# A fused Mamba-2 scan and low-rank mixer on one core: sums moved from GpSimd to VectorE, one tile's Strassen product made plain, dummy products merged, and weight loads held back

## The chip, the cores and the metric

The kernel runs on one NeuronCore of a Trainium2 chip. The metric is device time in microseconds (us) of one execution, as the median of several. Beside it stands the profile of one execution on the same kind of core, with the start and duration of every instruction on every engine: TensorE (PE, with its weight loads shown apart as PEld), VectorE (DVE), ScalarE (ACT), GpSimd (POOL), and the DMA issues of SyncE (SP). "Span" is the time from the first to the last instruction in that profile.

## What is computed

Two stages follow each other, in fp32. First a chunked state-space scan over 4 batches, 8 heads, 768 positions, head size 32 and state size 16:

```python
L = np.exp(cum[..., :, None] - cum[..., None, :]) * causal
y_intra = einsum('bhij,bhjd->bhid', (Cc @ Bc.T) * L, xc)
y_inter = einsum('bhin,bhnd->bhid', Cc, state) * exp(cum)[..., None]
state = exp(sum(la)) * state + sum_j(Bc_j xc_j * exp(cum[-1] - cum_j))
```

Then the heads are laid side by side, which gives x of 4 x 768 x 256, and a mixer with a residual follows:

```python
u = x + ((x.T @ U @ V).T)                 # mixing over the 768 positions, rank 32
out = u + np.maximum(u @ w_ch1, 0) @ w_ch2   # 256 -> 1024 -> 256
```

U, V and the two weight matrices arrive as 64-bit floats.

## The kernel before

**Staging.** The 768 positions of a batch are cut into 6 blocks of 128, taken as 3 pairs, so there are 12 pairs in all, numbered k = 0 to 11. For one pair the steps are `prep` (B and C times their decays, on DVE), `decayed` (POOL), `turn` (transposes to channel-major, copied out by ACT), `gram` (the C·B products, into four PSUM banks), `mask` (DVE, four pieces), `state` and `update` (the carried state; DVE, then POOL for the copy `Sm`), `inter` and `intra` (the two parts of y), `yout` (ACT), and `ytokens` (transposes back to position-major, copied out to `ytok`). After the three pairs of a batch the mixer of that batch runs: `project` (U), `mixed` (V, adds into u), then the product with w_ch1 and relu into `gT`, then the product with w_ch2 into `o` and the store, in three row tiles j = 0, 1, 2. The scan of batch b+1 runs between the pieces of batch b's mixer.

**Order.** The kernel opens a manual schedule: each engine runs its instructions in the order in which they are written. `plan`, `ups` and `downs` are lists of closures, and the main loop over k = 3 to 12 runs a list (`pieces`) between the steps of the scan.

**The two ways of multiplying.** For batch 0 the first product is plain: `up(k, m)`, two 128x384 products each, 16 of them. For batches 1 to 3 it is a seven-product Strassen scheme, `quad`, with pieces p1 to p7. It needs combined weights `ws`. The second product, `down(j)`, is Strassen for every batch: seven products of four 128x128 steps, with combined weights `w2s` and four DVE/POOL combinations S of the activations, made by `sums` (line 671). `operands` (line 922) makes `w2s` and `ws`, eight tensor ops of 128x512, on POOL, after the pairs k = 3, 4 and 5.

**Weights.** They are loaded as 64-bit words and turned into fp32 by `to_fp32`, in two halves of DVE and ACT instructions. `convert_ahead` runs the second half of one weight tile and the first half of the next; ten calls are spread by hand over the first part of the program. Tiles are U, V, four quarters of w1 (512 KB each) and four quarters of w2. All loads are issued by SP in one order: three pairs of B, C and x; U; V; w1's quarters; pair 3; w2's quarters; pairs 4 to 11. Six `words` buffers are shared, so that w2's loads wait for conversions.

**Dummy products.** `warm` and `fill` put products of the identity with itself, 128x128 each, in front of chosen steps, so that TensorE stays active during the first pairs, where it has little to do.

**Extra edges.** `behind` remembers an ACT or DVE instruction, and `inter(k, 1)` is made to wait for it.

## Time and profile before

| what | value |
|---|---|
| time, median of 3 | 256.12 us (255.63 to 256.95) |
| span of the profiled execution | 253.7 us |
| mean TensorE clock granted | 0.992 |
| PE busy | 234.6 us |
| DVE busy | 151.9 us |
| ACT busy | 96.1 us |
| POOL busy | 50.3 us |

The shares are averages over quite different stretches. In the first 25 us three pairs of batch 0 are scanned while data and weights arrive. From 35 to 70 us the weights are converted while batch 0's first product and batch 1's scan run. After 100 us batches 1 to 3 run the same pattern.

### The profile page before, as it was taken

What the parts mean: (1) busy time and instruction counts of PE and PEld (TensorE: products, weight loads), DVE (VectorE), ACT (ScalarE), POOL (GpSimd) and SP (SyncE); (2) the same over time, 40 slices, a digit from 0 to 9 for tenths busy, and PEclk for the clock granted to TensorE, in tenths of its full rate; (3) what the DMA queues carried; (4) which work ended last, traced back from release to release, by engine and by line L of the source; (5) the groups of instructions that cost most, each with busy time, mean ns of one, the idle gap of its engine ahead of it and who ended that gap; (6) DMA issues with size and microseconds to landing.
All of it is one profiled execution on the core that took longest, in us unless ns stands there. A gap on an engine that the chain in (4) does not pass through costs nothing.

```text
span 253.7 us, 7506 instructions
## 1 busy us (share of the span) xinstructions
PE 234.6 (92%) x3222; PEld 180.9 (71%) x3222; DVE 151.9 (60%) x337; ACT 96.1 (38%) x248; POOL 50.3 (20%) x74
## 2 busy tenths in 40 slices
PE   7988689797978979999989999999999999999995
PEld 7866556454768868656579979565599986558995
DVE  3366579969697986257584935265582462447521
ACT  5345457557521301347532301536522113563110
POOL 4031000103471480004270200005320000051000
PEclk9999799999999999999999999999999999999999
DMA  6989796999875401100000110100001011000111
GB/s 79 113 120 285 126 276 118 128 111 102 99 97 64 88 1 44 41 0 4 0 5 0 48 40 4 41 3 1 3 3 44 3 41 41 3 0 0 41 45 41
DMA packets 81637, 14.60 MB, mean 58 GB/s; under 512 B 76036, under 2 KB 79556, under 8 KB 81604
## 3 DMA queue, kind: packets, MB, share of 16 engines
q1 hardware_dynamic: 81604, 14.13, 30.9%
q8 instruction: 25, 0.41, 0.7%
q14 instruction: 8, 0.07, 0.1%
HBM read 10.98 MB, written 3.15 MB: 56 GB/s over the span
## 4 chain that ended last, share of the span: by engine, by line
PE 77%; DVE 13%; ACT 4%; issue 3%; DMA 1%; POOL 0%; DVEq 0%; SPq 0%; POOLq 0%; ACTq 0%
PE x L682 16%; PE x L579 12%; PE z L682 11%; PE z L579 8%; PE y L498 4%; DVE words L671 3%; PE y L478 3%; PE x L216 2%; PE w L359 2%; PE w L537 2%; PE w L519 2%; PE x L377 2%; DVE yT L552 1%; PE x L548 1%; PE w L409 1%
## 5 line engine op out<-in xcount | busy, mean ns | idle before, releaser
L579 PE MATMUL x<-t,ws 128*128 128x384 f32 x72 | 29.2, 503 | 0.5 <-ACT top L584 0.5
L436 POOL TENSOR_TENSOR Sm<-S,slot 128x256 f32<-128x256 f32 (+1 forms) x12 | 9.8, 813 | 99.2 <-DVE S L429 83.3
L682 PE MATMUL x<-w2s,words 128*128 128x128 f32 x192 | 25.5, 275 | 0.0
L682 PEld LDWEIGHTS x<-w2s,words 128*128 128x128 f32 x192 | 23.6, 193 | 0.1
L579 PEld LDWEIGHTS x<-t,ws 128*128 128x128 f32 x72 | 12.4, 189 | 13.5 <-ACT top L584 4.9
L740 ACT COPY o<-x 128x128 f32<-128x128 f32 x12 | 3.2, 266 | 45.9 <-PE x L682 45.9
L567 ACT ACTIVATE gT<-gT 128x384 f32<-128x384 f32 x36 | 17.6, 523 | 5.9 <-DVE gT L588 5.3
L671 POOL TENSOR_TENSOR words<-gT 128x256 f32<-128x256 f32 (+1 forms) x12 | 8.2, 682 | 48.4 <-PE x L579 36.3
L671 DVE TENSOR_TENSOR words<-gT 128x512 f32<-128x512 f32 (+1 forms) x20 | 16.8, 839 | 0.6 <-ACT gT L567 0.6
L389 DVE TENSOR_TENSOR M<-x,causal 128x256 int32<-128x256 int32 x24 | 10.1, 420 | 11.5 <-PE z L377 11.4
L343 POOL TENSOR_TENSOR bd<-bc,FD 128x256 f32<-128x256 f32 (+1 forms) x13 | 9.9, 772 | 29.9 <-ACT FD L264 29.9
L682 PE MATMUL x<-w,gT 128*128 128x128 f32 x96 | 14.0, 287 | 1.8 <-issue 1.1
L682 PEld LDWEIGHTS x<-w,gT 128*128 128x128 f32 x96 | 11.9, 191 | 4.6 <-DVE yT L552 2.5
L682 PE MATMUL z<-w,words 128*128 128x128 f32 x96 | 12.8, 276 | 1.9 <-DVE words L671 1.9
L588 DVE TENSOR_TENSOR gT<-z,top 128x384 f32<-128x384 f32 x12 | 6.7, 558 | 11.2 <-PE z L579 9.3
L622 DVE TENSOR_SCALAR gT<-x 128x384 f32<-128x384 f32 x12 | 6.7, 558 | 11.1 <-PE x L579 11.1
L510 ACT COPY yT<-y 128x256 f32<-128x256 f32 x24 | 7.8, 377 | 14.3 <-PE y L478 14.3
L682 PE MATMUL z<-w2s,words 128*128 128x128 f32 x96 | 12.7, 276 | 0.5 <-DVE words L671 0.5
L682 PEld LDWEIGHTS z<-w,words 128*128 128x128 f32 x96 | 11.7, 192 | 2.1 <-DVE words L671 2.1
L682 PE MATMUL z<-w,gT 128*128 128x128 f32 x96 | 12.7, 275 | 0.0
L682 PE MATMUL x<-w2s,gT 128*128 128x128 f32 x96 | 12.7, 275 | 0.0
L642 PE MATMUL x<-yT,w 128*128 128x384 f32 x32 | 12.0, 496 | 0.7 <-DVE yT L552 0.6
(159 smaller groups left out, 527.2 us busy)
## 6 DMA issues: line engine op xcount, KB each, us to landing
words<-in_moe_w_ch_dram SPq DMA_DIRECT2D x8, 512.0 KB, 6.3
x<-in_x_dram SPq DMA_DIRECT2D x24, 128.0 KB, 3.3
out_dram<-o SPq DMA_DIRECT2D x11, 256.0 KB, 2.1
bc<-in_B_dram SPq DMA_DIRECT2D x24, 64.0 KB, 3.8
bc<-in_C_dram SPq DMA_DIRECT2D x24, 64.0 KB, 3.3
words<-in_moe_U_dram SPq DMA_DIRECT2D x1, 192.0 KB, 4.9
words<-in_moe_V_dram SPq DMA_DIRECT2D x1, 192.0 KB
out_dram<-o SPq DMA_DIRECT2D x1, 128.0 KB, 1.7
```

The lines of the kernel that those rows point to most:

```text
L343: nc.gpsimd.tensor_tensor(out=st[k]["bd"][:, c:c + n].rearrange("p c h n -> p (c h) n"), in0=bc_sb[k][:, 0, c:c + n].rearrange("p c h n -> ...
L389: done = nc.vector.tensor_tensor(out=M[:, r].bitcast(INT32).rearrange("p c s i -> p (c s) i"), in0=g[r].bitcast(INT32).rearrange("p c s i ...
L436: nc.gpsimd.tensor_tensor(out=s["Sm"][:, sl], in0=s["S"][:, sl].rearrange("p i (s d) -> p i s d", s=2), in1=slot[:, None, :, None].to_broa ...
L478: product = nc.tensor.matmul(out=y[p][ts(r % 2, H), r // 2, c], lhsT=own[ts(r, Q)], rhs=s["T"][ts(r, Q), 1, c, ts(p, H)], start=fresh(k, p ...
L498: nc.tensor.matmul(out=y[p][ts(i, Q), n, c], lhsT=x_sb[k][half, c, h], rhs=s["M"][half, h // 2, c, h % 2], start=fresh(k, p, [i]), stop=Tr ...
L510: nc.scalar.copy(out=yp[:, :, :, p], in_=st[k]["y"][p])
L567: nc.scalar.activation(g, g, AF.Relu)
L579: nc.tensor.matmul(out=X[name], lhsT=lhsT[:, ts(i, P)], rhs=rhs, start=start, stop=True, skip_group_check=True)
L588: nc.vector.tensor_tensor(out=g, in0=X[of], in1=X[other], op=ALU.add)
L642: nc.tensor.matmul(out=g, lhsT=w1[:, n, ts(m, P)], rhs=uT[:, n, ts(k, HS)], start=(n == 0), stop=(n == NCB - 1))
L671: engine.tensor_tensor(out=S[v][:, lo:hi], in0=l[:, lo:hi], in1=r[:, lo:hi], op=op)
L682: nc.tensor.matmul(out=X[name], lhsT=lhsT[:, i], rhs=rhs[:, i], start=start and u is None and i == 0, stop=True, skip_group_check=True)
```

## The change

It does six things. Dummy products of one call become one wide product. The loads from w1's third quarter on, and thus everything queued behind them on SP, wait for the last mask piece of pair 2. The j = 0 tile of batch 0's second product is made plain (`whole`: for each half, two transposes and eight 128x256 products, then one ACT copy), so it needs neither `w2s` nor S; `ahead` goes with it. `sums` and `operands` are all on DVE. The copy to `ytok` for batch 1 moves from DVE to ACT. And the hand-written order of batch 0 changes: conversions and `keep` move, all ten conversions end ahead of the main loop, and one set of two `up` products moves from the loop to before it. The purpose is that TensorE waits less for its operands, for GpSimd, and for loads.

```diff
+    def idle(t, n):
+        while n > 0:
+            m = min(n, max(t.shape[1] // P, 1), 4)
+            w = min(P, t.shape[1])
+            nc.tensor.matmul(out=t[:, :m * w].rearrange("p (m i) -> p m i", i=w), lhsT=ident,
+                             rhs=ident[:, None, :w].to_broadcast([P, m, w]), start=True, stop=True)
+            n -= m
...
-        for _ in range(fills[0]):
...
-            nc.tensor.matmul(out=flat[:, :n], lhsT=ident, rhs=ident[:, :n], start=True, stop=True)
+        if fills[0]:
+            idle(t if len(dims) == 1 else t.rearrange(
...
-    for k in range(DF // quarter):
-        load_words(w1[:, :, ts(k, quarter)],
+    held = [load_words(w1[:, :, ts(k, quarter)],
...
-        copy = nc.scalar.copy if b == 0 else nc.vector.tensor_copy
+        copy = nc.scalar.copy if b < 2 else nc.vector.tensor_copy
...
-                        engine = nc.gpsimd if b and j == 0 and lo < 3 else nc.vector
-                        engine.tensor_tensor(out=S[v][:, lo:hi], in0=l[:, lo:hi],
+                        nc.vector.tensor_tensor(out=S[v][:, lo:hi], in0=l[:, lo:hi],
...
+            def whole(k):
+                g = bank("x", DM)
+                for n in range(NCB):
+                    nc.tensor.matmul(
+                        out=g[:, ts(n, P)], lhsT=uT[:, n, ts(HT * k + j, P)], rhs=ident,
+                        is_transpose=True, start=(n == 0), stop=False, skip_group_check=True)
+                for half in range(2):
+                    for i in range(NM // 2):
+                        m = half * NM // 2 + i
+                        nc.tensor.matmul(out=g, lhsT=blocks()[k][half][:, i], rhs=w2[:, m],
+                                         start=False, stop=(m == NM - 1), skip_group_check=True)
...
+            if b == 0 and j == 0:
+                return sums, [lambda: whole(0), lambda: whole(1)]
...
-            plan = [[ups.pop(-2), ups.pop()], [ups.pop(-2), ups.pop()], downs.pop(0)]
+            plan = [[ups.pop(-2), ups.pop()]] + [[piece] for piece in downs.pop(0)]
...
-                plan[1].insert(2 * v, step(0, v, 0, 2))
-                plan[1].append(step(0, v, 2, 4))
+                plan[1].insert(6 + 2 * v, step(0, v, 0, 2))
+            plan[1] += [step(0, v, 2, 4) for v in range(4)]
...
-    mask(2, (1, 3))
+    tc.add_manual_dep(held[2].ins, mask(2, (1, 3)).ins.name, mybir.DependencyInfo(
+        mybir.DependencyClass.Sync, mybir.DependencyReason.DATA))
...
-    for _ in range(3):
+    for _ in range(2):
         some(2)
         convert_ahead()
     decays(others, "y")
     keep(others)
     prep(3)
     decayed(3)
+    some(2)
+    convert_ahead()
+    some(2)
+    convert_ahead()
+    prep(4)
+    decayed(4)
     some(2)
     turn(3)
     convert_ahead()
...
     update(3)
-    prep(4)
-    decayed(4)
+    convert_ahead()
     some(2)
     turn(4)
-    convert_ahead()
-    plan[0].append(convert_ahead)
...
-                pieces = pieces[:4] + tokens + pieces[4:]
+                pieces = pieces[:3] + tokens + pieces[3:]
...
-                          + late[11:] + (plan[0] if k < last else []))
+                          + late[11:] + [lambda: operands(4, nc.vector)] + (plan[0] if k < last else []))
...
-        if k == NPR + 1:
-            run(ahead)
-        if k < 2 * NPR:
-            operands((2, 2, 4)[k - NPR], nc.gpsimd)
+        if k < NPR + 2:
+            operands(2, nc.vector)
```

More of the change, by code (lines that the diff above doesn't have):

```diff
@@ L75 @@
     fills = [0]
+    def idle(t, n):
[5 more added lines that the diff above has]
+            n -= m
     def bank(tag, *dims):
         t = psum.tile([P, *dims], FP32, tag=tag, name=tag, bufs=BANKS[tag])
-        for _ in range(fills[0]):
-            flat = t if len(dims) == 1 else t.rearrange(
-                {2: "p a b -> p (a b)", 3: "p a b c -> p (a b c)"}[len(dims)])
-            n = min(P, flat.shape[1])
-            nc.tensor.matmul(out=flat[:, :n], lhsT=ident, rhs=ident[:, :n], start=True, stop=True)
+        if fills[0]:
+            idle(t if len(dims) == 1 else t.rearrange(
+                {2: "p a b -> p (a b)", 3: "p a b c -> p (a b c)"}[len(dims)]), fills[0])
         fills[0] = 0
@@ L144, in load_words @@
         t = words_of(dst)
-        nc.sync.dma_start(out=t.rearrange("p (i j) -> p i j", i=i), in_=src)
+        return nc.sync.dma_start(out=t.rearrange("p (i j) -> p i j", i=i), in_=src)
     U2, V2, w12, w22 = (w.bitcast(INT32) for w in (moe_U, moe_V, moe_w_ch1, moe_w_ch2))
@@ L155 @@
     quarter = WCOLS // NCB
-    for k in range(DF // quarter):
-        load_words(w1[:, :, ts(k, quarter)],
-                   w12[:, ts(k, 2 * quarter)].rearrange("(c p) m -> p c m", p=P))
+    held = [load_words(w1[:, :, ts(k, quarter)],
+                       w12[:, ts(k, 2 * quarter)].rearrange("(c p) m -> p c m", p=P))
+            for k in range(DF // quarter)]
     load_bc(3)
@@ L212, in warm @@
     def warm(n, tag="w"):
-        t = bank(tag, P)
-        for _ in range(n):
-            nc.tensor.matmul(out=t, lhsT=ident, rhs=ident, start=True, stop=True)
+        idle(bank(tag, 4 * P), n)
     warm(3, "x")
@@ L393, in mask @@
             behind.setdefault("part", done)
+        return done
     def chunks(k, c, n):
@@ L669, in sums @@
                     if v in which:
-                        engine = nc.gpsimd if b and j == 0 and lo < 3 else nc.vector
-                        engine.tensor_tensor(out=S[v][:, lo:hi], in0=l[:, lo:hi],
-                                             in1=r[:, lo:hi], op=op)
+                        nc.vector.tensor_tensor(out=S[v][:, lo:hi], in0=l[:, lo:hi],
+                                                in1=r[:, lo:hi], op=op)
             def times(name, tag, lhsT, rhs, start=True, u=None):
@@ L745, in p4 @@
                 del hold["o"]
+            def whole(k):
[9 more added lines that the diff above has]
+                                         start=False, stop=(m == NM - 1), skip_group_check=True)
+                to(k, 0)
+                behind.setdefault("part", nc.scalar.copy(out=hold["o"][:, k], in_=g))
+                if k:
+                    store(None, None)
+                    del hold["o"]
+            if b == 0 and j == 0:
+                return sums, [lambda: whole(0), lambda: whole(1)]
             return sums, [p1, p5, p6, p3, p7, p2, p4]
@@ L780, in mixer @@
         downs = [piece for pieces in downs for piece in pieces]
-        return project, mixed, ups, plan, downs, [step(0, v) for v in range(4)]
+        return project, mixed, ups, plan, downs
     halves = [half for w in weights for half in (to_fp32(*w),) * 2]
@@ L813 @@
     ytok[0] = mix.tile([P, NC, DM], FP32, tag="ytok", name="ytok")
-    project, mixed, ups, plan, downs, ahead = mixer(0)
+    project, mixed, ups, plan, downs = mixer(0)
     decays(one)
@@ L900 @@
     update(3)
-    prep(4)
-    decayed(4)
+    convert_ahead()
     some(2)
     turn(4)
-    convert_ahead()
-    plan[0].append(convert_ahead)
+    assert not halves
     ws = const.tile([P, 5, DF // 2], FP32)
@@ L933 @@
             if q:
-                pieces = pieces[:4] + tokens + pieces[4:]
+                pieces = pieces[:3] + tokens + pieces[3:]
             else:
                 late = downs
-                project, mixed, ups, plan, downs, _ = mixer(b - 1)
+                project, mixed, ups, plan, downs = mixer(b - 1)
                 pieces = (late[:1] + tokens + late[1:7] + [project] + late[7:11] + [mixed]
-                          + late[11:] + (plan[0] if k < last else []))
+                          + late[11:] + [lambda: operands(4, nc.vector)] + (plan[0] if k < last else []))
         if k == last:
```

## The prediction

> **What bounds the kernel now.** I read the page's busy times first, then who waits for whom on TensorE, then the idle stretches by window, then the timeline around each.

> ```profile
> PE 234.6 (92%) x3222; PEld 180.9 (71%) x3222; DVE 151.9 (60%) x337; ACT 96.1 (38%) x248; POOL 50.3 (20%) x74
> q8 instruction: 25, 0.41, 0.7%
> ```

> TensorE sets the end, so a saving is either PE work or PE idle time. The idle is 19.1 us of 253.7 in all. PE's own waits, longest first:

> ```profile
> PE x L443 <- issue: 2.4, 1, 2.4
> PE z L682 <- DVE words L671: 2.3, 2, 1.9
> PE w L359 <- ACT gT L647: 1.9, 1, 1.9
> PE x L216 <- POOL ident masks.py:199: 1.4, 1, 1.4
> PE x L678 <- DVE o L696: 1.3, 1, 1.3
> PE w L359 <- DVE BC L331: 1.3, 1, 1.3
> PE x L682 <- issue: 1.1, 1, 1.1
> ```

> All but the fourth lie where the change works. The two "issue" waits have no semaphore behind them. The 25 packets of queue 8 are 16 KB each; their start times in the trace give the cause. By count of PE records (6498), PE stood idle after its 962nd (25.18 us) and after its 3778th (130.01 us), exactly 11 x 256 apart: these are ends of blocks of 256 instructions. [...] PE can go on some 1.35 us after it ends. At 130 us: block entered 127.62, packet 128.58 to 129.81, PE on at 131.16. At 25 us: block entered 20.33, but the packet started only at 25.22, with all four quarters of w1 already in the DMA rings. The windows show what follows (columns: PE, PEld, DVE, ACT, POOL busy, clock, DMA share):

> ```profile
> 25.20:27.60 2.40, 0.00 (x0) 0.00 (x0) 2.33 (x8) 1.04 (x3) 0.00 (x0) 1.00 1.03 252
> 27.60:31.20 3.60, 3.58 (x109) 2.97 (x113) 0.83 (x3) 1.32 (x5) 0.00 (x0) 0.54 0.52 55
> 47.60:49.60 2.00, 0.10 (x2) 0.08 (x2) 1.97 (x5) 0.76 (x3) 0.88 (x1) 1.00 0.97 96
> 60.80:62.20 1.40, 0.13 (x2) 0.10 (x2) 1.40 (x3) 1.34 (x4) 0.00 (x0) 1.00 1.05 99
> 92.60:94.00 1.40, 0.10 (x2) 0.09 (x2) 1.40 (x3) 0.00 (x0) 1.40 (x2) 1.00 0.00 0
> ```

> The stall costs twice: 2.45 us of nothing, then 3.4 us at half the clock. In the next two gaps DVE is full. In the last one, and at 75 us, DVE is full because POOL slows it:

> ```profile
> 72.85 1.71 POOL L922 TENSOR_TENSOR w2s<-w 128x512 f32<-128x512 f32 x1
> 73.36 1.75 DVE L671 TENSOR_TENSOR words<-gT 128x512 f32<-128x512 f32 x1
> 74.53 1.70 POOL L922 TENSOR_TENSOR w2s<-w,w2s 128x512 f32<-128x512 f32 x1
> 75.03 1.74 DVE L671 TENSOR_TENSOR words<-gT,words 128x512 f32<-128x512 f32 x1
> ```

> The same DVE instruction alone takes 0.69 us.

> [...] the clock record here has half clock from 27.86 for 3.413 us. [...]

> **The change, part by part.**

> *Merged dummies.* The columns stay, PE time too; 13 products fewer, so 52 instructions fewer, which moves block ends. Worth nothing by itself.

> *Held loads.* Behind the waiting load on SP stand w1's last quarters, pair 3, all of w2, pairs 4 to 11. The mask it waits for ended at 24.5; those loads were issued from 18.7. At 25 us the rings then hold only w1's first half, which at the 285 GB/s of that slice is through by about 22.7. The block is entered at about 21.3 (the packet's earlier place, 52 instructions on), so the packet can end by about 24.0 and PE go on at 25.4, about when it arrives. Gain: 2.45 plus the half clock. For the latter I take 1.4, not 1.7 (half of 3.41), since intra(2) took 1.19 us against 0.79 and `project` kept a similar ratio. ACT gives 0.35 back: `ytok` of pair 2 then waits for it. Net -3.5: the first `up` product starts at 32.15 instead of 35.66. Do the late loads starve anyone? The third quarter must be there when its conversion begins, 33.7 in the new time. Released at 24.5, two quarters (1 MB at 285 GB/s, 3.7 us) land near 30; pair 3 (0.5 MB in small pieces at about 110 GB/s, 4.5 us) by 33; w2's first three by 38.5 to 39. Its first is converted from 38.8 on, its second from 42.9. It fits, with 2 us to spare.

> *Order in batch 0.* DVE then sets the pace: 7 conversions of 2.6, mixed 2.5, own/kept 0.8, prep, masks, update 3.7 = 25 us from 31.25, where it begins `mixed` in the new time. PE has 16 `up` products of 1.29 = 20.6, decays 1.35, turns and gram 2.6 = 24.6. With `keep` and the preps ahead of the conversions, PE need not wait for BC: the gaps 1.90 and 1.27 go, -3.17.

> *Plain tile.* Removed: 28 products of 0.223 (eight records last 0.89) = 6.24. Added: 16 of 128x256. No row has this width; a 128x384 product takes 0.645, so between 0.223 and 0.645, linear 0.434, x16 = 6.94. PE +0.70. But p5 and p3's wait for S goes (0.45 and 1.85): -2.30. Four S sums vanish on DVE too.

> *`operands` on DVE.* 8 x 0.69 = 5.5 us on DVE beside PE work (after pairs 3 and 4, and before batch 1's quads, each ready 0.5 us before its product), but POOL no longer doubles DVE's times: the gaps 1.30 and 0.23 at 92.6 and 85.4 go, -1.53.

> *Sums of batches 1 to 3 on DVE.* 20 of 128x256 (0.73 on POOL; on DVE about 0.38, between 0.29 for 128x128 and 0.69 for 128x512) and 4 of 128x128: eight each in batches 1 and 2, eight in batch 3. In batches 1 and 2 three go ahead of the relu at L622, where DVE idled 1.38: 1.15 fits. The last four delay the masks by 0.75, `inter` by 0.15, twice. In batch 3 four sit between two evacuations; p4 waits for the second of them and comes 0.9 late.

> *`ytok` on ACT.* ACT is idle 4 to 6 us there; nothing.

> *Block ends elsewhere.* With 100 instructions fewer, the end at 130 us falls among long products: -1.15. Now the block from `inter(5)` to `state(6)` lies wholly in dense small products (256 in 2.3 us) while the pair loads still run (packets 1 to 2.3 late): a stall of 0 to 1.5; I take 0.7.

> Sum: -3.5 - 3.17 - 2.30 + 0.70 - 1.53 - 1.15 = -10.95. Given back: 0.7 + 0.9 + 0.3, and 0.6 for gram waiting on ACT behind conversions: +2.5. Net -8.45: 256.12 - 8.45 = 247.7 us.

> **The rivals.**
> - *The block still comes late at 25 us, or another stalls as long:* the 3.5 us stay. For: every engine still holds w1's first half, and the margin is under 0.3 us. Against: half the bytes. 251.2 us.
> - *DVE becomes the bound in batches 1 to 3:* it takes 8 x 0.38 twice and 4 x 0.38 + 4 x 0.29, 8.8 us of sums, in stretches where it evacuates PSUM. If PE waits for half, 4.4 in place of 1.2: 250.9 us. Against: DVE idles over 1 us before most of these.
> - *The held loads starve the conversions (slower):* if all of w2 comes as late as it is issued, 5.8 us, and DVE waits for it, the start gained is lost and the stage ends 5.8 later: 256.1 + 5.8 less the later gaps (2.30 + 1.53 + 1.15 less 0.7 of product), about 257.6. For: two quarters and pair 3 stand ahead. Against: before, w2's issue was set by free buffers (SP waited 6.4 us for one), not by 18.7.
> - *No new waits:* 245.2 us.

> **How the numbers follow.** My forecast, with the last as its lower edge: 0.68. Stall stays: 0.13. DVE bound: 0.12. Starved: 0.07. Range 244.8 to 251.7 holds the forecast and the two middle rivals. Slower by over 0.5%: 0.06; within: 0.03; faster: 0.91.

> **What would show it.** Right: no "issue" wait over 0.5 us near 25 us, clock 1.0 from 25 to 35, first `up` at about 32, batch 1's first quad at about 94 (before 103.4), no gap over 0.5 us before L682's successors near 65 to 92, 128x256 products at 0.43. Wrong: a half-clock window anywhere, an issue gap near 72 over 1.5 us, PE waiting on conversions with DVE waiting on DMA from 33 to 50, or PE waiting over 1 us per batch on DVE in the quads.

## The result, and the profile after

| | before | after |
|---|---|---|
| time, median of 4 | 256.53 us (255.63 to 258.85) | 246.18 us (244.90 to 250.28) |
| ratio, 95% interval | | 0.9565 (0.949 to 0.964) |
| span of the profiled execution, mean clock | 253.7 us, 0.992 | 242.8 us, 1.0 |

The 250.28 us is one execution at a mean clock of 0.986; this ratio, and every ratio below, leaves out executions more than 1.5% above the fastest of the same kernel. Measured again later, the changed kernel took 246.73 us, 0.963 (0.957 to 0.968) of the kernel before it.

The busy times and the instruction queue of the changed kernel, from its page:

```profile
PE 231.8 (95%) x3172; PEld 176.2 (73%) x3172; DVE 154.0 (63%) x359; ACT 97.4 (40%) x249; POOL 23.4 (10%) x42
q8 instruction: 25, 0.41, 0.7%
```

POOL lost 27 us and DVE gained only 2: four sums are left out with the plain tile, and DVE's sums no longer run beside POOL's (0.68 us each at 72.63 and 73.23, before 1.75 and 1.74). PE's last product ends 10.9 us earlier. Of this, 8.1 us are waits that PE no longer has: its idle time up to that product is 8.1 us, before 16.2. The other 2.8 us are busy time, up to 1.7 of it the half clock (half of its 3.41 us). PE's waits in the changed kernel (total, times, longest):

```profile
PE x L82 <- POOL ident masks.py:199: 1.4, 1, 1.4
PE x L382 <- ACT gT L653: 1.1, 1, 1.1
PE w L415 <- issue: 1.0, 1, 1.0
...
PE x L585 <- DVE gT L594: 0.5, 1, 0.5
```

Of the six waits of before that lay where the change works, all are gone. Two of about one microsecond are new: `gram` of pair 3 behind ACT (L382), and an end of an instruction block in `state` of pair 6 (L415). The five windows shown of before, in the changed kernel (same columns, and at the end the GB/s that the DMA engines moved):

```profile
25.20:27.60 2.40, 2.35 (x95) 1.99 (x94) 2.37 (x8) 1.59 (x6) 0.00 (x0) 1.00 0.92 297
27.60:31.20 3.60, 3.10 (x33) 1.66 (x31) 2.34 (x5) 3.22 (x8) 0.00 (x0) 1.00 0.93 153
47.60:49.60 2.00, 1.89 (x7) 0.76 (x5) 1.99 (x5) 2.00 (x6) 0.00 (x0) 1.00 0.97 142
60.80:62.20 1.40, 1.40 (x19) 1.23 (x10) 1.21 (x6) 0.65 (x2) 0.10 (x1) 1.00 0.97 99
92.60:94.00 1.40, 1.40 (x13) 1.27 (x12) 1.15 (x3) 0.19 (x1) 0.00 (x0) 1.00 0.00 0
```

PE was idle or at half clock in all five; now it is busy in all, at full clock, although DVE is at least as full as before in the first three, and DMA is over 0.9 busy in them. And the sums that took 1.75 us beside POOL, from the timeline of the changed kernel:

```profile
72.63 0.68 DVE L676 TENSOR_TENSOR words<-gT 128x512 f32<-128x512 f32 x1
73.23 0.68 DVE L676 TENSOR_TENSOR words<-gT,words 128x512 f32<-128x512 f32 x1
```

Where the time came from, by the start of the first product of each stage in the two traces:

| stage | before | after | change | forecast |
|---|---|---|---|---|
| start to first `up` | 35.66 | 31.53 | -4.13 | -3.5 |
| first `up` to batch 1's first `quad` | 67.75 | 62.08 | -5.67 | -5.0 |
| batch 1's to batch 2's first `quad` | 55.08 | 53.65 | -1.43 | -1.0 |
| batch 2's to batch 3's first `quad` | 52.83 | 52.53 | -0.30 | +0.15 |
| batch 3's first `quad` to PE's end | 39.53 | 40.17 | +0.64 | +0.9 |
| sum | 250.85 | 239.96 | -10.9 | -8.45 |

The forecast column adds up the prediction's terms by stage (-5.0 is -3.17 - 2.30 + 0.70 - 1.53 + 0.7 + 0.6). Every stage came out 0.3 to 0.7 us better than forecast.

### The profile page after: what moved, and what is told of

Same layout as the page of the kernel before. It is cut to its first block, busy times and chain, and to the rows that moved or that the text cites. A ratio compares the mean times of both kernels' runs of the same rounds, so it can differ in the third digit from the quotient of the medians.

```text
span 242.8 us, 7387 instructions
## 1 busy us (share of the span) xinstructions
PE 231.8 (95%) x3172; PEld 176.2 (73%) x3172; DVE 154.0 (63%) x359; ACT 97.4 (40%) x249; POOL 23.4 (10%) x42
## 4 chain that ended last, share of the span: by engine, by line
PE 82%; DVE 6%; ACT 4%; SPq 3%; issue 2%; DMA 1%; POOL 0%; DVEq 0%; POOLq 0%; ACTq 0%
PE x L687 17%; PE x L585 13%; PE z L687 12%; PE z L585 9%; PE y L504 3%; PE y L484 3%; PE x L762 3%; SPq L117 3%; PE x L82 2%; PE w L543 2%; PE w L525 2%; DVE words L676 2%; PE x L382 2%; PE w L364 2%; DVE yT L558 2%
## 5 line engine op out<-in xcount | busy, mean ns | idle before, releaser
L687 PE MATMUL x<-w2s,words 128*128 128x128 f32 x176 | 23.2, 275 | 0.0
L687 PEld LDWEIGHTS x<-w2s,words 128*128 128x128 f32 x176 | 21.6, 193 | 0.0
L676 DVE TENSOR_TENSOR words<-gT 128x512 f32<-128x512 f32 (+2 forms) x30 | 17.4, 579 | 0.6 <-ACT gT L573 0.6
L348 POOL TENSOR_TENSOR bd<-bc,FD 128x256 f32<-128x256 f32 (+1 forms) x13 | 10.9, 842 | 24.7 <-DMA bc<-in_B_dram 18.6
L687 PE MATMUL x<-w,gT 128*128 128x128 f32 x88 | 12.6, 285 | 0.6 <-DVE yT L558 0.6
L687 PEld LDWEIGHTS x<-w,gT 128*128 128x128 f32 x88 | 10.8, 191 | 3.2 <-DVE yT L558 2.5
L435 DVE SCALAR_TENSOR_TENSOR S<-S,kept,w 128x64 f32<-128x64 f32 x40 | 11.2, 279 | 1.7
L594 DVE TENSOR_TENSOR gT<-z,e 128x384 f32<-128x384 f32 x12 | 6.7, 557 | 7.9 <-PE z L585 5.6
L648 PE MATMUL z<-yT,w 128*128 128x384 f32 x32 | 11.6, 486 | 0.0
L687 PE MATMUL z<-w,words 128*128 128x128 f32 x88 | 11.6, 275 | 0.0
L687 PE MATMUL z<-w,gT 128*128 128x128 f32 x88 | 11.6, 275 | 0.0
```

Of the source, the lines that this page charges most:

```text
L348: nc.gpsimd.tensor_tensor(out=st[k]["bd"][:, c:c + n].rearrange("p c h n -> p (c h) n"), in0=bc_sb[k][:, 0, c:c + n].rearrange("p c h n -> ...
L435: done = nc.vector.scalar_tensor_tensor(out=new, in0=st["S", b], scalar=kept[:, b, j, None], in1=add, op0=ALU.mult, op1=ALU.add)
L594: nc.vector.tensor_tensor(out=g, in0=X[of], in1=X[other], op=ALU.add)
L648: nc.tensor.matmul(out=g, lhsT=w1[:, n, ts(m, P)], rhs=uT[:, n, ts(k, HS)], start=(n == 0), stop=(n == NCB - 1))
L676: nc.vector.tensor_tensor(out=S[v][:, lo:hi], in0=l[:, lo:hi], in1=r[:, lo:hi], op=op)
L687: nc.tensor.matmul(out=X[name], lhsT=lhsT[:, i], rhs=rhs[:, i], start=start and u is None and i == 0, stop=True, skip_group_check=True)
```

## The experiments

Each was timed beside the kernel before, and ratios are to that. Where the changed kernel is compared, its ratios are the two above. "Block" means 256 of PE's records, weight loads counted: the two "issue" stalls of the kernel before lie 11 x 256 records apart, and that of the changed kernel, by its own count, 6 x 256 records after the place of the first of them. "Packet" means one of the 25 of queue 8, 16 KB each. PE went on from these three stalls 1.35 to 1.52 us after the end of one; that a packet brings the next block of instructions is an inference from this and from the counts (25 packets to 6498 records).

**The hold, taken out of the changed kernel and added alone to the one before.**

```diff
-    tc.add_manual_dep(held[2].ins, mask(2, (1, 3)).ins.name, mybir.DependencyInfo(
-        mybir.DependencyClass.Sync, mybir.DependencyReason.DATA))
+    mask(2, (1, 3))
```

> The changed kernel with the loads no longer held: from w1's third quarter on they are issued as soon as their buffers allow. My theory (the DMA rings, full of w1's four quarters, keep the instruction packet late): the issue wait near 24 to 25 us is back with 1.5 to 2.5 us, a half-clock window of 3.4 us follows it, and the time is 249.2 to 250.2 us against 246.2. Rival (the merged dummy products moved the end of the block, and that alone took the stall away): no issue wait over 0.5 us near 25 us, 246 to 246.7 us.

Measured: 250.71 us, ratio 0.975 (0.969 to 0.980). The packet starts at 25.12 us (held: 22.88), PE stands for 1.70 us at 25.71, and the windows show the half clock behind it:

```profile
24.00:27.60 3.60, 1.90 (x61) 1.38 (x67) 3.53 (x14) 1.60 (x5) 0.20 (x1) 0.98 1.00 272
27.60:31.20 3.60, 3.60 (x94) 2.83 (x86) 1.53 (x4) 1.82 (x4) 0.00 (x0) 0.55 0.51 55
```

In the first line DMA is full (1.00) and PE busy only 1.90 of 3.60; in the second the clock is 0.55. So the hold is what takes the stall at 25 us away, as the theory said, and merging alone does not. But the time lost is not all lost there. PE's waits show three stalls:

```profile
PE y L504 <- issue: 3.1, 2, 1.7
...
PE w L415 <- issue: 1.4, 1, 1.4
```

The second, of 1.41 us at 63.20, is not in the changed kernel; the third, of 1.38 us at 79.33, is followed by another stretch of half clock. The first `up` product starts 3.35 us later than in the changed kernel, and the rest comes after it. One execution at full clock took 247.87 us, 1.6 to 3.0 us more than the changed kernel at full clock (244.90 to 246.25).

The other way round, the kernel before with the hold and the same edge:

> The kernel before with nothing but the hold added. My theory: the stall of 2.45 us at 25 us and the half-clock window go, the first up product starts near 32 us instead of 35.66, and the time is 3.5 us lower, 253.0 us, if the start gained is not lost again to conversions that wait for data. Rival (held loads starve the conversions): DVE waits for w2's words between 33 and 55 us, and under 1.5 us are left, 255 us or more.

Measured: 254.75 us, ratio 0.990 (0.984 to 0.995). By the ratio this is 2.7 us (1.2 to 4.2), so the time alone does not rule out the 3.5 us expected. The profile, of an execution of 256.18 us, does not have that gain: its first `up` product starts at 36.42 us, in the kernel before at 35.66. Nor is the rival's reason in it. The stall at 25 us is gone, but PE's waits have another:

```profile
PE w L538 <- issue: 2.1, 1, 2.1
```

It lies at 30.11 us, at the end of the next block. That block was entered at 25.59, and its packet started only at 29.90, after the held loads had been issued from 24.91 on (DMA 0.95 busy from 27.6 to 31.2). Half clock follows at 32.04. In this execution the stall was moved by one block. Two others ran at full clock throughout (251.92 and 253.32 us), so they had no half clock; whether they had the stall is not on record.

**The merged dummies, undone in the changed kernel and made alone in the one before.**

```diff
-        if fills[0]:
-            idle(t if len(dims) == 1 else t.rearrange(
...
+        for _ in range(fills[0]):
...
+            nc.tensor.matmul(out=flat[:, :n], lhsT=ident, rhs=ident[:, :n], start=True, stop=True)
```

> The changed kernel with one dummy product per 128 columns again: the same columns, 52 PE instructions more, so every later end of an instruction block comes 52 instructions earlier in the program. Theory 1 (merging is worth nothing by itself, ends of blocks decide): the block that stalled 1.05 us at 75 us no longer lies wholly in small products, that wait goes, but the next one (17% fewer records between pair 4's gram and inter) may stall near 67 us with up to 1 us; 245.1 to 246.3 us. Theory 2 (merged products bring the clock up earlier, as the full clock from 5.9 us instead of 7.4 suggests): everything before 24 us comes 0.7 us later, 246.0 to 247.0 us, and full clock begins near 7.4 us.

Measured: 249.05 us, ratio 0.972 (0.968 to 0.977), some 2.5 to 4 us more than the changed kernel. Neither theory had it. PE's timeline, unmerged:

```profile
29.25 0.41 PE L547 MATMUL w<-ytok,U_sb 128*32 128x128 f32 x5 [0.20 <-ACT ytok L532]
31.21 0.63 PE L547 MATMUL w<-ytok,U_sb 128*32 128x128 f32 x11 [1.55 <-issue]
```

and merged, the changed kernel:

```profile
28.77 0.64 PE L543 MATMUL w<-ytok,U_sb 128*32 128x128 f32 x16 [0.20 <-ACT ytok L528]
```

Unmerged, the block ends after five of the last sixteen records of `project`, where PE arrives at 29.66 us, before the packet has even ended (28.78 to 29.75). Merged, the packet is as late (28.68 to 29.66), but the block ends 52 instructions further on, among the first `up` products, which PE reaches only at about 32. That is the same block end as in the profile of the kernel with the hold alone. The stall at 75 us did go, as theory 1 said; another of 1.14 us stands at 72.23 in its place, as the theory had feared for 67. The half clock came once, at 54.82, after the wait of `gram` for ACT.

> The kernel before with nothing but the dummy products merged: 52 PE instructions fewer. Theory 1: the stall at 130 us (1.15 us) goes, since its block no longer lies wholly in small products; the one at 25 us moves later by some 1 us and stays 1 to 2.5 us long, since the DMA rings are as full as before; 254.5 to 256 us. Theory 2 (an earlier clock too): a further 0.7 us lower before 24 us, full clock from about 5.9 us. Rival (the end of the block at 25 us moves out of the trouble by itself): no issue wait near 25 us, 252 us or less.

Measured: 256.99 us, ratio 0.998 (0.995 to 1.002). The stall at 130 us is gone, the one at 25 us is longer (3.34 us, packet at 26.50), and one of 1.33 us is new at 65.37. Merging alone is worth nothing that the interval shows. The full clock did begin early here, at 6.05 us, but it did so at 5.71 us in a kernel with unmerged dummies too (below), and at 6.98 in the one without the hold, whose dummies are merged: the start of full clock varies by itself, and theory 2 falls.

**The two new waits of the changed kernel.** The reference for these is the changed kernel once more:

> The changed kernel unaltered, as the mark for the three variants beside it: 245 to 247 us. The gaps of 1.15 us (gram of pair 3) and 1.05 us (state of pair 6) are there again if they are the program's own; a half-clock window of 3.41 us may come or stay out[...].

Measured: 246.73 us (245.63 to 247.48). Gaps of 1.02 us at 49.82, 1.17 at 74.70, and 0.58 at 106.14.

```diff
+            cut = 2 if 2 <= m < 4 else 1
             for n in range(NCB):
-                nc.tensor.matmul(out=g, lhsT=w1[:, n, ts(m, P)], rhs=uT[:, n, ts(k, HS)],
+                for h in range(cut):
+                    nc.tensor.matmul(out=g[:, ts(h, HS // cut)], lhsT=w1[:, n, ts(m, P)],
+                                     rhs=uT[:, n, HS * k + HS // cut * h:HS * k + HS // cut * (h + 1)],
```

> The changed kernel with the columns of four up products (m = 2 and 3 for both k) done in two halves of 192: the same work in 32 more instructions, between 33 and 46 us. Block theory: no block of 256 instructions lasts under 3 us any more, the wait of 1.05 us at the state of pair 6 goes and no other takes its place; 8 more products cost about 0.1 us; the time is 0.9 us lower than the changed kernel's, 1.7 more where the wait had brought on a half-clock window. Rival (the wait has another cause, such as the transfers of the pairs): it stays within 0.2 us of 1.05, and the time is 0 to 0.2 us higher.

Measured: 245.42 us, ratio 0.958 (0.952 to 0.964). PE at pair 6, split:

```profile
74.18 0.86 PE L504 MATMUL y<-M,x 64*32 64x64 f32 x64
76.25 0.57 PE L415 MATMUL w<-x,bd 64*32 64x64 f32 x32 [1.21 <-issue]
```

and in the changed kernel:

```profile
74.17 0.45 PE L415 MATMUL w<-x,bd 64*32 64x64 f32 x15
75.67 0.35 PE L415 MATMUL w<-x,bd 64*32 64x64 f32 x17 [1.05 <-issue]
```

The block end moved as meant, ahead of `state` instead of into its middle, and its block lasted about 4.2 us instead of 2.0. The stall stayed: the packet started at 73.92 us, 3.1 us after the block was entered. In the changed kernel it started at 73.19, 0.5 us after. So the packets come at nearly the same time, although one block was entered 1.8 us earlier than the other, and a longer block alone is no cure: the block theory of this wait falls. The gap at 106 us did go. The median is 1.3 us lower although the stall stayed; three of the six executions of the changed kernel beside it, and two of these six, had a mean clock below 0.995.

```diff
     turn(3)
-    convert_ahead()
     some(2)
     gram(3)
...
     update(3)
-    convert_ahead()
+    prep(5)
+    decayed(5)
     some(2)
     turn(4)
+    convert_ahead()
+    convert_ahead()
```

> The changed kernel with the conversions around pair 3's gram moved behind its masks, and pair 5's prep ahead of them, so that the relu copies no longer stand behind conversions on ACT. Theory (ACT's order makes gram wait): the gap of 1.15 us at gram of pair 3 shrinks to 0.3 or less and no new one over 0.3 follows up to 62 us; 0.8 to 1.0 us lower than the changed kernel. Rival (DVE sets the pace of this stage anyhow): the time comes back as a wait for BC or for w2's last quarter before 65 us, and under 0.3 us are left.

Measured: 245.57 us, ratio 0.959 (0.954 to 0.964). The gap at `gram` of pair 3 is gone and no other over 0.2 us lies between 33 and 74 us: the place of the conversions was the cause. That it is their part on ACT, and not that on DVE, rests on the releaser that the profile names (ACT `gT`). The block stall came with 0.83 us, and one of 0.60 us at 25.57. The gain by medians is 1.2 us, within the spread of single runs.

> Both edits together: the two gaps are independent, so the gains add, 1.7 to 1.9 us below the changed kernel, 243.5 to 245 us. Rival (one brings the other back, by moving the transfers against the blocks): under 1.0 us.

Measured: 245.03 us, ratio 0.955 (0.950 to 0.960); each of its six runs (244.24 to 245.50) lies below each of the six of the changed kernel measured beside it. The gain of 1.7 us is as expected in size, but not in its parts: the gap of gram fell to 0.21 and the one at 106 us went, while the stall at 75 us grew to 1.49. Three of the changed kernel's six runs had a mean clock of 0.993 and none of these, which is part of the difference.

**What delays the packet at 75 us.** On top of that version, pair 10's loads wait for pair 6's last mask:

```diff
+            done = mask(k + 1)
+            if k == 5:
+                tc.add_manual_dep(later.ins, done.ins.name, mybir.DependencyInfo(
+                    mybir.DependencyClass.Sync, mybir.DependencyReason.DATA))
```

> The variant with split and swapped steps, with pair 10's loads (and everything behind them on SP) held until pair 6's last mask at about 75 us. Theory (a packet comes late because the small pieces of pair 10's B and C stand ahead of it in the DMA engines; a longer block alone did not help): packet 8 starts by 72.5 us in place of 73.9 to 74.1, and the wait at the state of pair 6 falls from 1.49 us to 0.3 or less; 243.8 to 244.3 us. Rival (the packet's delay has nothing to do with these loads): packet 8 starts at 73.5 us or later and the wait stays over 1 us, 245 us.

Measured: 244.47 us, ratio 0.957 (0.952 to 0.961), with the shortest profiled span of all, 241.5 us. SP's queue in this kernel, and then PE:

```profile
67.73 1.18 SPq L129 DMA_DIRECT2D x<-in_x_dram  x2
74.66 0.37 SPq L118 DMA_DIRECT2D bc<-in_B_dram  x1
```

```profile
74.12 0.57 PE L420 MATMUL w<-x,bd 64*32 64x64 f32 x32 [0.38 <-issue]
```

No load is issued from 69 to 74.7 us, the packet starts at 71.92 instead of 74.14, and the stall falls from 1.49 to 0.38 us, a little more than was expected to be left. About half of the 2.2 us is the loads' doing: the block itself was entered 1.16 us earlier (69.55 instead of 70.71), and the packet's delay after that fell from 3.43 to 2.38 us. So the held loads explain 1.05 us of the delay, and with it nearly all of what the stall lost. Whether it is the small pieces of B and C or the loads of x behind them was not separated. The median differs too little from 245.03, measured at another time, to call this version faster than the one before it.

**The engine of the sums and operands.**

```diff
+                        engine = nc.gpsimd if b and j == 0 and lo < 3 else nc.vector
...
-        if k < NPR + 2:
-            operands(2, nc.vector)
+        if k < 2 * NPR:
+            operands((2, 2, 4)[k - NPR], nc.gpsimd)
```

> The changed kernel with the sums of tile j = 0 and the operands back on POOL, where and as the kernel before had them. Theory (POOL slows DVE[...]): waits for DVE and POOL return in the quads of batch 1 and ahead of tile 0 of batches 1 and 2, 1.5 to 2.5 us in all, 248 to 249 us. Rival (without batch 0's sums nothing on DVE is in the way at 70 to 93 us any more, so the engine does not matter): under 0.5 us, 246.3 to 246.9 us.

Measured: 244.08 us, ratio 0.958 (0.953 to 0.963): as fast as the changed kernel. DVE's sums beside POOL are slow again (1.64 and 1.75 us, in the changed kernel 0.68), and it costs little:

```profile
69.44 1.71 POOL L954 TENSOR_TENSOR w2s<-w 128x512 f32<-128x512 f32 x1
```

```profile
70.06 1.64 DVE L677 TENSOR_TENSOR words<-words,gT 128x512 f32<-128x512 f32 x1
71.62 1.75 DVE L677 TENSOR_TENSOR words<-gT 128x512 f32<-128x512 f32 x1
```

PE waits 0.38 us for masks on DVE at 74 us and 0.37 for ACT at 76 us, not 1.53 in all; the 0.53 us that batch 3 had paid for DVE's sums are saved; and the block stall at 75 us stayed away, since its packet came at 70.73 us, though the block is as short as in the changed kernel (2.0 us). Why the packet came earlier was not found, so the absence of that stall, 1.05 us, cannot be credited to POOL. That DVE's sums are slower beside POOL was right, the time put on it was not.

**The plain tile alone, in the kernel before** (`whole` as in the change, and no `ahead`):

> The kernel before with tile 0 of batch 0's second product made plain and nothing else. Theory: 0.70 us more of PE work, the waits for S (0.45 and 1.85 us) go, and since 47 PE instructions fewer move the later blocks, the stall of 1.15 us at 130 us goes too: 2.7 us lower, 253.6 us. Rival (the waits for S only give way to waits for w2's last conversion or for the transfers): under 1.0 us lower.

Measured: 252.18 us, ratio 0.988 (0.983 to 0.993), 3.3 us by medians. The waits for S and the stall at 130 us are gone, as the theory had it; the others stand, with 6.8 us of half clock after the first:

```profile
PE x L443 <- issue: 2.8, 1, 2.8
PE w L359 <- ACT gT L647: 1.9, 1, 1.9
...
PE x L678 <- DVE o L696: 1.3, 1, 1.3
PE w L359 <- DVE BC L331: 1.3, 1, 1.3
```

**Batch 0's order, undone in the changed kernel** (the lines between the first `some(2)` and `turn(4)` as before, four `up` products in the loop):

> The changed kernel with batch 0's order of before: keep and the preps of pairs 3 and 4 behind the conversions, four up products in the loop. Theory: the waits of the transposes of pairs 3 and 5 for BC return (1.90 and 1.27 us before), the wait of gram of pair 3 for ACT (1.0 to 1.15 us) changes or goes: 2.0 to 3.2 us more than the changed kernel, 248.5 to 249.8 us. Rival (DVE has the same work in either order and sets the pace, so the wait only moves): within 0.7 us of the changed kernel.

Measured: 250.31 us, ratio 0.976 (0.970 to 0.982). Its runs at a mean clock of 1.0 took 247.86 to 249.48 us, about 3 us more than those of the changed kernel (244.90 to 246.25, both times it was measured). The two waits are back to the tenth:

```profile
PE w L364 <- ACT gT L653: 1.9, 1, 1.9
...
PE w L364 <- DVE BC L336: 1.3, 1, 1.3
```

The gap at `gram` of pair 3 is not there; block stalls of 1.34 us at 65.27 and 0.64 at 83.83 are, and in the profiled run one of 1.47 at 21.95.

## Why the prediction was right, and where not

The forecast of 247.7 us, made for 256.12, lies 1.5 us above the 246.18 measured: a gain of 8.45 us where 10.35 came. The direction and most causes were right. One sign that had been set for "wrong" shows outside the profiled execution: mean clocks of 0.993 and 0.986 in other executions of the changed kernel are one and two stretches of half clock (half of 3.41 us is 0.7% of 245).

- *Held loads* (-3.5): measured -4.13 at the first `up`. Without the hold the stall and the half clock return, with later stalls (3.0 to 4.6 us in all, by the ratios). The packet times were as forecast: start 22.88, end 23.97 (about 24.0), next block reached at 25.25 without a wait. The reason given for them was too simple: w1's first half was not through by 22.7, its loads landed at 23.18 and 24.47, so the packet did not wait for all that stood ahead of it. That it waits behind loads in the DMA rings at all was my inference from the times of issue, landing and packet; the trace shows no rings. ACT's `ytok` gave back 0.20 (0.35). No conversion waited for its words. Some 0.7 us of the surplus is not the change's: everything up to 24 us is 0.73 us earlier, after a full clock that began at 5.89 instead of 7.38 us. Over these kernels that start lies anywhere from 5.4 to 8.1 us, with merged and unmerged dummies alike.
- *Merged dummies* (nothing by itself): right alone (ratio 0.998), but the step was wrong in what it left out. I followed the packet at 25 us and not the next one, which starts 3.4 us after its block is entered in the changed kernel and 4.3 us after it with the hold alone. The 52 instructions put that block's end where PE arrives after the packet. That the -3.5 held was luck in this respect: undoing the merge in the changed kernel costs 2.4 to 4.0 us by the ratios (0.972 instead of 0.957 to 0.963).
- *Order in batch 0* (-3.17): right. 1.89 and 1.29 us return when it is undone. The first of the two the profile puts down to ACT (`gT`), the prediction to BC; before, the two end 0.04 us apart (49.45 and 49.41), so the profile does not tell which one PE needed last.
- *Plain tile* (+0.70 of products, -2.30 of waits): the waits went. The product's price was right (eight in 3.46 us, 0.4325 each; forecast 0.434), but the Strassen side was priced too low: it took 7.65 us with its transposes, from 71.06 to 81.44 less the waits and `ytokens`, the plain one 3.89 and 3.90. So +0.14 instead of +0.70.
- *Operands on DVE* (-1.53): the gaps went, but not for that reason. With the operands and sums back on POOL neither returns; two other waits, of 0.75 us together, come at 74 and 76 us. The likeliest cause is that DVE no longer copies `ytok` (0.69 us at 86.28 before), which I had costed at nothing; the new order of batch 0 is another candidate. Neither was tried alone.
- *Sums of batches 1 to 3 on DVE* (+0.3 and +0.9): a sum of 128x256 took 0.42 us on DVE (forecast 0.38), yet no delay of masks shows in batches 1 and 2; two waits of 0.26 us for ACT went instead. In batch 3 PE waits 0.53, and on POOL that wait is gone.
- *Block ends elsewhere* (-1.15, +0.7): the one at 130 us went (also with the merge or the plain tile alone), the new one came where it was forecast, with 1.05. My reason, a block wholly in small products, is half of it: a block of 4.2 us stalled as well, and a block of 2.0 us with an early packet did not. In these runs the time of the packet decided (73.92 us in the long block, 70.73 in the short one with POOL), and the length of the block only how soon it was needed; holding the loads from pair 10 on cut the stall to 0.38.
- *gram behind ACT* (+0.6): measured 1.15, and gone when ACT's order is changed.

Of the rivals, "the stall stays" is what the hold met in the profiles without the merge (2.06 us at 30.11 alone, 1.55 at 29.66 in the changed kernel).

## What to carry to other kernels

Here every idle stretch of TensorE of 0.5 us or more that had no semaphore behind it lay at the end of a block of 256 instructions and ended 1.2 to 1.6 us after a packet: find the packet's start and what the DMA engines were doing, and then look at the next packets too, since here the hold moved the burst onto the next one (started at 28.68 us, 3.4 us after PE had entered its block). Count, too, where the following block ends fall: in the changed kernel 52 instructions more, the products unmerged, cost 2.4 to 4.0 us, though merging alone gained nothing that shows. A slower engine is not yet a cost: here DVE's sums took 1.64 to 1.75 us beside POOL instead of 0.68, and the kernel was as fast (244.08 us). Put the operation back and see whether anything waits.

## What the runs showed of the hardware

**An instruction packet came later beside loads.** In the order of PE's records, weight loads counted, all 22 stretches marked "issue" of 0.5 us or more in these profiles come, within one record, after record 194 or a multiple of 256 further, and in all of them PE went on 1.2 to 1.6 us after the end of a packet (1.39 and 1.35 in the kernel before, 1.52 in the changed one). Where no DMA engine was busy, a packet started up to 2.4 us after PE had entered its block (114.71 to 117.09 us with batch 0's old order), and sometimes ahead of that (by 2.05 us in the kernel before, 218.98 against 221.03). Beside loads it took up to 6.0 us (55.74 to 61.74 in the kernel without the hold, DMA 0.97 busy), in the kernel before 4.89 (20.33 to 25.22, 0.98). Every delay over 2.4 us lies in a stretch with the DMA engines at least 0.8 busy. All profiled kernels but two had such a stall of 0.5 us or more; in those two, the one with pair 10's loads held and the one with POOL, the longest was 0.38 and 0.3.
